# One choice of experts over nine columns instead of two over four and five, and one copy moved in front of the square root, in an attention and mixture-of-experts kernel

## The chip, the cores and the metric

The kernel runs on one core of a Trainium2 chip. Its engines are TensorE (PE in the profile; its weight loads are PEld), VectorE (DVE), ScalarE (ACT), GpSimd (POOL) and SyncE (SP, which here only issues DMAs). Each engine works through its own list of instructions in order and waits for the others by semaphores. The metric is the device time of one execution in microseconds; the number compared is the median over several runs.

## The reference

Linear attention with a norm is followed by a layer of eight experts, in which every expert takes exactly as many tokens as any other:

```
kv  = einsum('bhsd,bhse->bhde', k, v)             # 8 batches, 8 heads, 576 rows, head size 64
out = einsum('bhsd,bhde->bhse', q, kv)
rms = sqrt(mean(out*out, -1) + 1e-6)
x   = (out / rms * g_norm) as (4608, 512)         # tokens x (heads * head size)

logits = x @ w_gate                               # 4608 x 8
for (tok, e) in order of falling logits:          # over all tokens and experts together
    skip if tok is assigned or expert e has 576 tokens
    assigned[tok] = e
out[tokens of e] = relu(x[tokens of e] @ w1[e]) @ w2[e]     # 512 -> 1024 -> 512
```

## The kernel before, in words

**Attention part.** For each batch `prepare` forms kv on TensorE, turns q and appends, behind each head's 64 columns of kv, the 8 columns of kv times w_gate; so one product gives a head's output and its share of the 8 logits. `tiles` then goes through the batch in tiles of 128 tokens. Batches alternate between four tiles and five (the fifth joins the last rows of two batches), so that the 4608 tokens stand in 36 *columns* of 128. For each tile TensorE writes `o_ps` in PSUM (L433), ACT squares it into `sq` (L439; two buffers) and copies it to `o_sb` (L441), and DVE sums the squares of each head into `ms` (L447). Behind the last tile of a batch ACT takes the root `rt` (L450), DVE makes `inv` out of it (L456 to L460), scales the logit shares to `part` (L462) and sums them to the logits `lg` of the batch's columns (L465). GpSimd scales the outputs of a batch into `xo` (L470), except in the last batch, where ACT does it in forty small operations (L475); SyncE writes `xo` to `x_dram`.

In the last batch the copies of tiles 2, 3 and 4 are put off: `keep` goes into the list `held_back` and runs behind the root.

**Choice of experts.** `early` is a generator for a group of columns: clip the logits (L237), take each token's highest (L240), mark and number the expert that has it (L242, L243, L245, L247), and compare the highest logit with 32 candidate thresholds (L303, `over_c`). It yields between these steps. The main loop puts the generator of each batch in the list `choices`, and while it works through the tiles of the next batch it takes steps out of it (`chosen`), by a table of numbers per tile. In the last batch the table is (0, 1, 1, 0, 0), and what remains of the choice of batch 6 is done behind the root by a loop of its own; the choice of batch 7 follows behind its logits.

**Search and experts.** For expert 0 `threshold` counts on TensorE, over all 36 columns, how many tokens lie above each candidate (L576; one weight load and one matmul a column), narrows the threshold on DVE and repeats, four rounds in all. Then the tokens of expert 0 are listed, 14 matmuls that compute nothing needed keep TensorE busy (`warm_ps`, L736), GpSimd gathers the rows of x (L793), TensorE transposes them (L874) and the eight experts follow, with products on TensorE, sums of operands on GpSimd (L896) and sums of results on DVE (L961).

**What sets the order.** Everything up to the first expert is recorded under a manual schedule: each of PE, DVE, ACT and SP gets its instructions in the order in which the code issues them. So where a line stands in the code, and at which tile a generator is stepped, is the engine's order. PSUM of the expert part takes the place of that of the attention part, so its first matmul (L576) waits until the last `o_ps` is copied.

The functions that the change touches, and what calls them:

Of the kernel before, what the change touches and what calls it, by code (L numbers as in the profile page):

```python
# [27 lines left out]
def kernel(  # L28
# [14 lines left out]
    B, H, S, D = q.shape  # L43
# [5 lines left out]
    R = S // HP  # L49
# [25 lines left out]
    def paced(dma):  # L75

        if len(issued) >= 2 * AHEAD:
            tc.add_manual_dep(dma.ins, issued[-AHEAD].name,
                              mybir.DependencyInfo(mybir.DependencyClass.Sync, mybir.DependencyReason.DATA),
                              reason="paced loads")  # L80
        issued.append(dma.ins)
# [146 lines left out]
    def choice(c0=None, c1=GC):  # L228


        cs = slice(c0 or 0, c1)
        n = cs.stop - cs.start
        m, cm, cd = (mx, code_mx, code) if c0 is not None else (small_ps[k] for k in ("mx", "code_mx", "code"))
        if c0 is None:
            nc.vector.tensor_tensor(wl, lg, bc_e(small_ps["shut"]), op=AL.add)
        else:
            nc.vector.tensor_scalar(lg[:, :, cs], in0=lg[:, :, cs], scalar1=bound, scalar2=bottom,  # L237
                                    op0=AL.min, op1=AL.max)
        w = wl if c0 is None else lg
        nc.vector.tensor_reduce(m[:, cs], w[:, :, cs].rearrange("p e c -> p c e"), axis=AXX, op=AL.max)  # L240
        yield
        nc.vector.tensor_tensor(pick[:, :, cs], w[:, :, cs], bc_c(m[:, cs]), op=AL.is_ge)  # L242
        nc.vector.tensor_tensor(pick[:, :, cs], pick[:, :, cs], bc_e(cd, n), op=AL.mult)  # L243
        yield
        nc.vector.tensor_reduce(cm[:, cs], pick[:, :, cs].rearrange("p e c -> p c e"), axis=AXX, op=AL.max)  # L245
        yield
        nc.vector.tensor_tensor(best[:, :, cs], pick[:, :, cs], bc_c(cm[:, cs]), op=AL.is_equal)  # L247
        if c0 is None:
            nc.vector.tensor_tensor(mx, m, gone, op=AL.add)
# [49 lines left out]
    def compare_thirds(over, cand, c0=0, c1=GC):  # L299
        for n in range(3):  # L300
            a, b = max(c0, n * THIRD), min(c1, (n + 1) * THIRD)
            if a < b:
                nc.vector.tensor_tensor(  # L303
                    over[n][:, a - n * THIRD:b - n * THIRD], mx[:, a:b].rearrange("p (c o) -> p c o", o=1).to_broadcast([P, b - a, NCAND]),
                    cand.rearrange("p (o n) -> p o n", o=1).to_broadcast([P, b - a, NCAND]), op=AL.is_ge)

    def early(c0, c1):

        yield from choice(c0, c1)
        yield  # L310
        compare_thirds(over0, cand0, c0, c1)
# [98 lines left out]
    def tiles(c0, rows, last=False):  # L410


        T = len(rows)
        o_sb = att.tile([P, T, H, W], FT, name="o_sb", tag="o_sb", bufs=2)
        xo = att.tile([P, T, H, D], FT, name="xo", tag="xo", bufs=LAG + 1)
        ms = att.tile([P, T * H], FT, name="ms", tag="ms")
        held_back = []
        for t, halves in enumerate(rows):


            in_kv = last and t == 2
            o_ps = psa.tile([P, 2, 512], FT, name="o_ps", tag="kv" if in_kv else "o", bufs=1 if in_kv else 2)
            for r2 in range(NP // 2):
                for l in range(2):
                    for rp in range(2):
                        r = 2 * r2 + rp
                        at = [slice(h * HP, (h + 1) * HP) for h in range(2)]
                        parts = [(slice(0, P), halves[0], 2)] if halves[0][0] == halves[1][0] else [
                            (at[n], half, 1) for n, half in enumerate(halves)]
                        for rows_at, (bn, j), m in parts:  # L430
                            block = R * r + j
                            ks = slice(block % 2 * D, (block % 2 + 1) * D)
                            nc.tensor.matmul(  # L433
                                o_ps[rows_at, rp, (2 * r2 + l) * W:(2 * r2 + l + 1) * W],
                                lhsT=turned_q[bn][ks, l, block // 2:block // 2 + m].rearrange("p x c -> p (x c)"),
                                rhs=kv_of[bn][ks, 2 * r + l], start=True, stop=True)
            o4 = o_ps[:, :, 0:NP * W].rearrange("p b (h w) -> p b h w", w=W)
            sq = att.tile([P, H, D], FT, name="sq", tag="sq")
            nc.scalar.activation(sq.rearrange("p (b h) d -> p b h d", b=2), o4[:, :, :, 0:D], ACT.Square, scale=D ** -0.5)  # L439
            def keep(t=t, o_ps=o_ps):  # L440
                nc.scalar.copy(o_sb[:, t].rearrange("p (b h) w -> p b (h w)", b=2), o_ps[:, :, 0:NP * W])  # L441

            if last and t > 1:
                held_back.append(keep)
            else:
                keep()
            nc.vector.reduce_sum(out=ms[:, t * H:(t + 1) * H], in_=sq, axis=AXX)  # L447
            yield
        rt = att.tile([P, T * H], FT, name="rt", tag="rt")
        nc.scalar.activation(rt, ms, ACT.Sqrt, bias=eps)  # L450
        while last and choices:
            chosen()
        for do in held_back:
            do()
        inv = att.tile([P, T * H], FT, name="inv", tag="inv")
        nc.vector.reciprocal(inv, rt)  # L456

        nc.vector.scalar_tensor_tensor(rt, in0=inv, scalar=-0.5, in1=inv, op0=AL.mult, op1=AL.mult)
        nc.vector.scalar_tensor_tensor(rt, in0=ms, scalar=EPS, in1=rt, op0=AL.add, op1=AL.mult)
        nc.vector.scalar_tensor_tensor(inv, in0=rt, scalar=1.5, in1=inv, op0=AL.add, op1=AL.mult)  # L460
        part = att.tile([P, T * H, E], FT, name="part", tag="part")
        nc.vector.tensor_tensor(  # L462
            part, o_sb[:, :, :, D:W].rearrange("p t h e -> p (t h) e"),
            inv.rearrange("p (a o) -> p a o", o=1).to_broadcast([P, T * H, E]), op=AL.mult)
        nc.vector.reduce_sum(out=lg[:, :, c0:c0 + T].rearrange("p e t -> p t e"),  # L465
                             in_=part.rearrange("p (t h) e -> p t e h", t=T), axis=AXX)

        for t in range(T):
            if c0 + T <= last_own:
                nc.gpsimd.tensor_tensor(xo[:, t], o_sb[:, t, :, 0:D],  # L470
                                        inv[:, t * H:(t + 1) * H].rearrange("p (h o) -> p h o", o=1).to_broadcast([P, H, D]),
                                        op=AL.mult)
            else:
                for h in range(H):
                    late.append(lambda t=t, h=h: nc.scalar.mul(xo[:, t, h], o_sb[:, t, h, 0:D],  # L475
                                                               inv[:, t * H + h:t * H + h + 1]))
        for x in range(0, T, 2):
            y = min(x + 2, T)
            writes.append(lambda x=x, y=y: paced(nc.sync.dma_start(
                x_dram[(c0 + x) * P:(c0 + y) * P, :].rearrange("(t p) f -> p t f", p=P),  # L480
                xo[:, x:y].rearrange("p t h d -> p t (h d)"))))

    def work(b):
        rows = [((b, j), (b, j + 2)) for j in (0, 1, 4, 5)]
        c = b // 2 * R + b % 2 * (R // 2)
        if b % 2:
            rows.append(((b - 1, R - 1), (b, R - 1)))
        column_of.update({c + t: row for t, row in enumerate(rows)})
        yield from tiles(c, rows, b + 1 == B)
        choices.append(early(c, c + len(rows)))  # L490

    choices, column_of = [], {}

    def chosen():

        if choices and next(choices[0], "all") == "all":
            choices.pop(0)
# [830 lines left out]
```

## Time and profile before

| | |
|---|---|
| median of 3 runs | 629.81 us (620.28 to 634.88) |
| profiled execution | 629.0 us, span 627.2 us from first to last instruction |
| granted TensorE clock, mean | 0.956 of full speed |
| PE busy | 591.6 us (94%) |
| PEld busy | 465.3 us (74%) |
| DVE busy | 373.5 us (60%) |
| ACT busy | 179.7 us (29%) |
| POOL busy | 412.9 us (66%) |
| DMA | 91.07 MB, mean 145 GB/s |

The busy shares are means over two unlike parts: the attention part up to about 123 us, and the experts from about 151 us to the end, where TensorE hardly pauses. Between them lies a stretch in which TensorE is mostly idle or does little. A row of the timeline gives the start in us, the duration, the engine, the line, the operation with what it writes and reads, how often, and in brackets how long the engine was idle before it and what ended that. A row of a group gives the busy time in all and the mean in ns of one.

### The profile page before, as it was taken

The page shows a single profiled execution, that of the slowest core. Times are in us where ns is not written, and L with a number is a line of the kernel's source. Part 1 is how long each engine was busy: PE and PEld are TensorE (multiplying, and loading weights), DVE is VectorE, ACT ScalarE, POOL GpSimd, SP SyncE. Part 2 cuts the span into 40 slices and gives each one's busy share as a digit, 9 for nine tenths or more (in the row PEclk, how much of TensorE's full clock was granted, in tenths as well). Part 3 has the DMA queues.
Part 4 walks back from the last instruction along what each step waited for, and adds up shares of the span by engine and source line. Part 5 has one row for each costly group of instructions (what it writes and reads, how often), then busy time and mean ns, then how long its engine had stood idle before and what let it go on. Part 6 is the DMA issues. An engine that isn't in the chain of part 4 may idle for free.

```text
span 627.2 us, 12012 instructions
## 1 busy us (share of the span) xinstructions
PE 591.6 (94%) x4644; PEld 465.3 (74%) x4644; DVE 373.5 (60%) x1172; ACT 179.7 (29%) x387; POOL 412.9 (66%) x367
## 2 busy tenths in 40 slices
PE   6899989638999999999999999999999999999996
PEld 3787877534788678867886787788678867877784
DVE  2535876877887797768746873786383146123511
ACT  1345765742221322122212321322122112212300
POOL 0034455304998989698769696967887799778323
PEclk9858999858999999999999999999999999999998
DMA  8996889827209154075036204610654053002002
GB/s 288 296 319 232 281 289 324 316 86 253 90 8 337 68 199 154 1 245 175 1 135 210 76 0 169 196 56 2 209 202 144 0 182 104 2 1 75 1 1 80
DMA packets 41410, 91.07 MB, mean 145 GB/s; under 512 B 3456, under 2 KB 3456, under 8 KB 41344
## 3 DMA queue, kind: packets, MB, share of 16 engines
q1 hardware_dynamic: 34752, 71.31, 33.3%
q0 software_dynamic: 5888, 18.88, 9.1%
q8 instruction: 39, 0.64, 0.4%
q14 instruction: 27, 0.22, 0.1%
q10 hardware_dynamic: 704, 0.02, 0.1%
HBM read 71.32 MB, written 18.87 MB: 144 GB/s over the span
## 4 chain that ended last, share of the span: by engine, by line
PE 85%; DVE 6%; issue 3%; DMA 2%; POOL 2%; ACT 1%; POOLq 0%; DVEq 0%; ACTq 0%
PE h_ps L966 33%; PE y_ps L1068 31%; PE o_ps L433 5%; PE y_ps L1082 4%; PE kv_ps L345 4%; PE t_ps L874 3%; PE qt_ps L330 2%; DVE ms L447 1%; PE warm_ps L736 1%; DMA v_sb<-in_v_dram 1%; PE given_ps L580 1%; DMA g_col<-in_g_norm_dram 1%; PE given_ps L576 1%; POOL out_dram L883 1%; PE begun_ps L268 0%
## 5 line engine op out<-in xcount | busy, mean ns | idle before, releaser
L966 PE MATMUL h_ps<-xt,w_sb 128*128 128x288 f32 x384 | 101.0, 412 | 0.9 <-ACT xt L877 0.8
L978 ACT ACTIVATE hid<-hid 128x288 f32<-128x288 f32 x128 | 55.7, 445 | 147.4 <-DVE hid L961 141.8
L966 PEld LDWEIGHTS h_ps<-xt,w_sb 128*128 128x128 f32 x384 | 70.8, 190 | 24.8 <-issue 5.7
L961 DVE TENSOR_TENSOR hid<-h_ps,u 128x288 f32<-128x288 f32 x128 | 56.8, 454 | 29.1 <-PE h_ps L966 25.0
L966 PE MATMUL h_ps<-sx,sw 128*128 128x288 f32 x256 | 67.9, 407 | 0.1
L793 POOL DMA_INDIRECT xg<-x_dram,ids x40 | 38.2, 955 | 34.9 <-DVE upper L633 22.6
L1068 PE MATMUL y_ps<-tw,sh 128*128 128x256 f32 x256 | 61.1, 383 | 0.0
L1068 PE MATMUL y_ps<-tw,hid 128*128 128x256 f32 x256 | 60.9, 381 | 0.0
L1068 PE MATMUL y_ps<-w_sb,hid 128*128 128x256 f32 x256 | 59.5, 382 | 0.0
L966 PEld LDWEIGHTS h_ps<-sx,sw 128*128 128x128 f32 x256 | 48.4, 190 | 13.9 <-DVE u L961 0.6
L877 ACT ACTIVATE xt<-t_ps,g_col 128x512 f32<-128x512 f32 (+1 forms) x40 | 25.8, 645 | 110.6 <-PE t_ps L874 110.5
L470 POOL TENSOR_TENSOR xo<-o_sb,inv 128x512 f32<-128x512 f32 x31 | 32.5, 1077 | 30.5 <-ACT sq L439 16.1
L1068 PEld LDWEIGHTS y_ps<-w_sb,hid 128*128 128x128 f32 x256 | 47.4, 190 | 6.4
L1068 PEld LDWEIGHTS y_ps<-tw,sh 128*128 128x128 f32 x256 | 47.3, 190 | 6.1
L1068 PEld LDWEIGHTS y_ps<-tw,hid 128*128 128x128 f32 x256 | 47.1, 190 | 6.0
L961 DVE TENSOR_TENSOR y_sb<-y_ps,u 128x512 f32<-128x512 f32 x24 | 16.5, 690 | 53.5 <-PE y_ps L1068 53.5
L961 DVE TENSOR_TENSOR u<-h_ps,u 128x288 f32<-128x288 f32 x96 | 41.9, 449 | 10.3 <-PE h_ps L966 8.1
L433 PE MATMUL o_ps<-kvx,qt 64*128 64x72 f32 (+1 forms) x640 | 43.7, 286 | 3.4 <-DVE kvx L396 2.4
L433 PEld LDWEIGHTS o_ps<-kvx,qt 64*128 64x128 f32 (+1 forms) x640 | 38.7, 194 | 8.2 <-issue 7.0
L896 POOL TENSOR_TENSOR sh<-hid 128x512 f32<-128x512 f32 x16 | 20.3, 1271 | 32.7 <-ACT hid L978 31.7
L896 POOL TENSOR_TENSOR tw<-w_sb 128x512 f32<-128x512 f32 x32 | 40.0, 1273 | 0.2
L376 POOL COPY kvx<-kv 64x512 f32<-64x512 f32 x16 | 9.8, 611 | 45.7 <-DVE kv L370 45.3
(214 smaller groups left out, 1093.5 us busy)
## 6 DMA issues: line engine op xcount, KB each, us to landing
w_sb<-in_moe_w_dram SPq DMA_DIRECT2D x16, 1024.0 KB, 6.2
w_sb<-in_moe_w_dram SPq DMA_DIRECT2D x8, 2048.0 KB, 13.8
k_sb<-in_k_dram SPq DMA_DIRECT2D x16, 576.0 KB, 5.2
v_sb<-in_v_dram SPq DMA_DIRECT2D x16, 576.0 KB, 5.8
q_sb<-in_q_dram SPq DMA_DIRECT2D x16, 576.0 KB, 6.0
x_dram<-xo SPq DMA_DIRECT2D x16, 512.0 KB, 3.8
x_dram<-xo SPq DMA_DIRECT2D x4, 256.0 KB, 4.4
xg<-x_dram,ids POOLq DMA_INDIRECT x40
```

Source lines behind the costliest of these rows:

```text
L345: nc.tensor.matmul(kv_ps[cs, l, r * D:(r + 1) * D], lhsT=k_sb[ls, r, j, :], rhs=v_sb[ls, r, j, :], start=(j < 2), stop=(j >= R - 2))
L433: nc.tensor.matmul(o_ps[rows_at, rp, (2 * r2 + l) * W:(2 * r2 + l + 1) * W], lhsT=turned_q[bn][ks, l, block // 2:block // 2 + m].rearrange ...
L470: nc.gpsimd.tensor_tensor(xo[:, t], o_sb[:, t, :, 0:D], inv[:, t * H:(t + 1) * H].rearrange("p (h o) -> p h o", o=1).to_broadcast([P, H, D ...
L793: tokens = nc.gpsimd.indirect_dma_start(out=xg[0:nr], out_offset=None, in_=x_dram, in_offset=bass.IndirectOffsetOnAxis(ap=ids[0:nr, n:n + ...
L874: nc.tensor.transpose(t_ps[:, d, 0:nr], xg[0:nr, d * P:(d + 1) * P], ident[0:nr, 0:nr])
L877: nc.scalar.mul(xt[:, :, a:a + nr], t_ps[:, :, 0:nr], g_col)
L896: in_order(nc.gpsimd.tensor_tensor(o, x, y, op=op))
L961: nc.vector.tensor_tensor(o, p_ps, u, op=AL.add)
L966: nc.tensor.matmul(o, lhsT=left[:, d, f * P:(f + 1) * P], rhs=right[:, d], start=d == 0, stop=d == KH - 1)
L978: nc.scalar.activation(h, h, ACT.Relu)
L1068: nc.tensor.matmul(p_ps[:, n], lhsT=left[:, f, n * P:(n + 1) * P], rhs=right[:, f], start=(f == 0), stop=(f == FH - 1))
L1082: nc.tensor.matmul(y_ps[l * nr:(l + 1) * nr], lhsT=hid[:, l * FH + f, a:a + nr], rhs=w2[:, l * FH + f, :], start=(f == 0), stop=(f == FH - 1))
```

## The change

```
@@ in tiles(), behind the loop over the tiles
             nc.vector.reduce_sum(out=ms[:, t * H:(t + 1) * H], in_=sq, axis=AXX)
             yield
+        if held_back:
+            held_back.pop(0)()
         rt = att.tile([P, T * H], FT, name="rt", tag="rt")
         nc.scalar.activation(rt, ms, ACT.Sqrt, bias=eps)
         while last and choices:
@@ in work(b)
         yield from tiles(c, rows, b + 1 == B)
-        choices.append(early(c, c + len(rows)))
+        if b + 2 < B:
+            choices.append(early(c, c + len(rows)))
+        elif b + 1 == B:
+            choices.append(early(c - R // 2, c + len(rows)))
```

`held_back` holds the copies of tiles 2, 3 and 4 of the last batch; the first of them now stands in front of the root. Batch 6 (`b + 2 == B`) no longer leaves a choice behind, so that the steps taken in batch 7 and the loop behind the root find nothing to do, and batch 7 makes one choice over the columns 27 to 35, the four of batch 6 and its own five.

On DVE, in the last batch, the order before runs from the first reduction (`ms`) to the first step of `inv`; `pick`, `code_mx`, `best` and `over_c` are steps of the choice of batch 6:

```order
L447 TENSOR_REDUCE ms<-sq 128x8 x2
L237 TENSOR_SCALAR lg<-lg,bound,bottom 128x8x4
L240 TENSOR_REDUCE mx<-lg 128x4
L447 TENSOR_REDUCE ms<-sq 128x8
L242 TENSOR_TENSOR pick<-lg,mx 128x8x4
L243 TENSOR_TENSOR pick<-pick,code 128x8x4
L447 TENSOR_REDUCE ms<-sq 128x8 x2
L245 TENSOR_REDUCE code_mx<-pick 128x4
L247 TENSOR_TENSOR best<-pick,code_mx 128x8x4
L303 TENSOR_TENSOR over_c<-mx,cand 128x128
L456 RECIPROCAL inv<-rt 128x40
```

The changed kernel, from the same place to the comparison with the candidates (lines from 449 on are two higher in it, later five):

```order
L447 TENSOR_REDUCE ms<-sq 128x8 x5
L458 RECIPROCAL inv<-rt 128x40
...
L464 TENSOR_TENSOR part<-o_sb,inv 128x320
L467 TENSOR_REDUCE lg<-part 128x5x8
L237 TENSOR_SCALAR lg<-lg,bound,bottom 128x8x9
L240 TENSOR_REDUCE mx<-lg 128x9
L242 TENSOR_TENSOR pick<-lg,mx 128x8x9
L243 TENSOR_TENSOR pick<-pick,code 128x8x9
L245 TENSOR_REDUCE code_mx<-pick 128x9
L247 TENSOR_TENSOR best<-pick,code_mx 128x8x9
L303 TENSOR_TENSOR over_c<-mx,cand 128x288
```

The five reductions now stand together, the seven instructions of the four-column choice are gone, and the seven behind `lg` are nine columns wide instead of five.

On ACT, in the last batch, from the third square to the late scaling, before:

```order
L439 ACTIVATE sq<-o_ps 128x512 x3
L450 ACTIVATE rt<-ms,eps 128x40
L441 COPY o_sb<-o_ps 128x576 x3
L475 ACTIVATE xo<-o_sb,inv 128x64 x40
L877 ACTIVATE xt<-t_ps,g_col 128x4x128 x3
```

And in the changed kernel:

```order
L439 ACTIVATE sq<-o_ps 128x512 x3
L441 COPY o_sb<-o_ps 128x576
L452 ACTIVATE rt<-ms,eps 128x40
L441 COPY o_sb<-o_ps 128x576 x2
L477 ACTIVATE xo<-o_sb,inv 128x64 x40
```

One of the three copies has moved from behind the root to in front of it. On TensorE, GpSimd and SyncE the order of the instructions is the same; the counting matmuls of the columns 27 to 30 now need the choice that is made behind `lg`.

More of the change, by code (lines that the diff above doesn't have):

```diff
@@ L448, in tiles @@
             yield
+        if held_back:
+            held_back.pop(0)()
         rt = att.tile([P, T * H], FT, name="rt", tag="rt")
@@ L489, in work @@
         yield from tiles(c, rows, b + 1 == B)
-        choices.append(early(c, c + len(rows)))
+        if b + 2 < B:
+            choices.append(early(c, c + len(rows)))
+        elif b + 1 == B:
+            choices.append(early(c - R // 2, c + len(rows)))
     choices, column_of = [], {}
```

## The prediction

> **What bounds the kernel now.** I read the page first, then the chain of waits, and then the timeline around the end of the attention part, where the edit lies.
>
> ```profile
> PE 85%; DVE 6%; issue 3%; DMA 2%; POOL 2%; ACT 1%; POOLq 0%; DVEq 0%; ACTq 0%
> ```
>
> The chain that ended last is TensorE for 85%, VectorE (DVE) for 6% and ScalarE (ACT) for 1%. So the edit, which changes only the order and widths of DVE and ACT instructions, can act only in a short piece of the span. The timeline shows that piece (columns: start, duration, engine, line, operation, count, and in brackets the idle time before it and what ended it):
>
> ```profile
> 116.17 4.19 POOL L470 TENSOR_TENSOR xo<-o_sb,inv 128x512 f32<-128x512 f32 x4 [3.79 <-ACT sq L439]
> ...
> 116.98 1.27 DVE L447 TENSOR_REDUCE ms<-sq 128x8 f32<-128x512 f32 x2
> ...
> 117.75 1.19 ACT L439 ACTIVATE sq<-o_ps 128x512 f32<-128x512 f32 x2
> ...
> 118.61 0.68 DVE L447 TENSOR_REDUCE ms<-sq 128x8 f32<-128x512 f32 x1
> ...
> 119.38 0.60 ACT L439 ACTIVATE sq<-o_ps 128x512 f32<-128x512 f32 x1 [0.45 <-DVE ms L447]
> 119.44 0.96 DVE L243 TENSOR_TENSOR pick<-pick,code 128x32 f32<-128x32 f32 x1
> ...
> 120.33 1.27 DVE L447 TENSOR_REDUCE ms<-sq 128x8 f32<-128x512 f32 x2
> ...
> 121.63 0.33 ACT L450 ACTIVATE rt<-ms,eps 128x40 f32<-128x40 f32 x1 [1.65 <-DVE ms L447]
> ...
> 121.86 1.70 ACT L441 COPY o_sb<-o_ps 128x576 f32<-128x576 f32 x3
> 122.06 0.40 DVE L456 RECIPROCAL inv<-rt 128x40 f32<-128x40 f32 x1
> ...
> 122.96 0.20 DVE L460 SCALAR_TENSOR_TENSOR inv<-rt,inv 128x40 f32<-128x40 f32 x1
> ...
> 123.60 0.49 DVE L462 TENSOR_TENSOR part<-o_sb,inv 128x320 f32<-128x320 f32 x1 [0.43 <-ACT o_sb L441]
> 123.61 0.98 PE L576 MATMUL given_ps<-best,over_c 128*32 128x8 bf16 x31 [4.93 <-ACT o_sb L441]
> ...
> 126.34 0.32 DVE L303 TENSOR_TENSOR over_c<-mx,cand 128x160 bf16<-128x160 f32 x1
> ...
> 126.71 0.30 PE L576 MATMUL given_ps<-best,over_c 128*32 128x8 bf16 x5 [2.12 <-DVE over_c L303]
> ...
> 128.86 1.43 PE L576 MATMUL given_ps<-best,over_c 128*32 128x8 bf16 x36 [1.44 <-DVE over_c L303]
> ```
>
> Two waits matter. The root (L450) sat 1.65 us until the last of the five reductions of batch 7 came from DVE; that DVE was late because the four-column choice of batch 6 stands between the reductions. Behind the root ACT makes three copies, and `part` (L462) waits 0.43 us for the last. TensorE is idle 4.93 us and then waits 2.12 us more for the choice of the last five columns. From there to the first product of expert 0 the chain is one dependent step after another, and TensorE runs nearly without a gap behind it. What is won or lost up to the matmuls at 126.71 therefore moves the end one for one, unless something on a clock of its own holds it back.
>
> **The reductions come together.** Two squares end at 117.75 + 1.19 = 118.94, so the third is ready at about 118.35 and the fourth at 118.94. Before, the third reduction begins at 118.61 and the last two at 120.33, with the multiply of the choice, 0.96 us long, ahead of them. Its groups by shape:
>
> ```profile
> L243 DVE TENSOR_TENSOR pick<-pick,code 128x32 f32<-128x32 f32 x4 | 2.7, 680 | 0.1
> L243 DVE TENSOR_TENSOR pick<-pick,code 128x40 f32<-128x40 f32 x4 | 0.8, 201 | 0.1
> L243 DVE TENSOR_TENSOR pick<-pick,held_ps 128x288 f32<-128x288 f32 x7 | 3.2, 454 | 0.2
> L240 DVE TENSOR_REDUCE mx<-lg 128x5 f32<-128x40 f32 x4 | 0.9, 224 | 0.1
> L240 DVE TENSOR_REDUCE held_ps<-wl 128x36 f32<-128x288 f32 x7 | 4.7, 672 | 0.2
> L303 DVE TENSOR_TENSOR over_c<-mx,cand 128x160 bf16<-128x160 f32 x3 | 1.0, 319 | 0.0
> L303 DVE TENSOR_TENSOR over_c<-mx,cand 128x384 bf16<-128x384 f32 x9 | 4.5, 554 | 0.1
> ```
>
> With 32 elements it takes 680 ns on average, with 40 only 201. The slow ones lie beside GpSimd's scaling of the tile before: here the multiply ends at 120.40, 0.04 us behind GpSimd's four operations (116.17 + 4.19 = 120.36). The reductions in that stretch keep their 0.68 and 0.64 us, so they aren't held up by it, and without the choice they close up. The third runs from about 118.43 to 119.11. The fifth square needs the buffer of the third and started 0.09 us behind that reduction (118.61 + 0.68 = 119.29, then 119.38); now it runs from 119.20 to 119.80. The fourth reduction fills 119.02 to 119.70, the fifth 119.88 to 120.56. The root follows the last reduction by 0.03 us as it does now (121.60, 121.63): **120.59 in place of 121.63, 1.04 us earlier.**
>
> **The copy in front of the root.** ACT is free at 119.80 and the root can't begin before 120.59. One copy takes 1.70 / 3 = 0.57 us, or at most the 0.63 of a lone one if the overlap is lost, and ends at 120.37 to 120.43: hidden by the fifth reduction, with some 0.2 us to spare. If that cover were gone it would cost the root up to 0.57. Behind the root stand two copies instead of three. They start 0.23 behind the root's start as now and end at 120.82 + 1.13 = 121.95 instead of 123.56. On the other side `inv` ends at 123.16 now and at 122.12 then. The wait of 0.43 for the copies is gone, and what is late next is `inv`: `part` starts at about 122.15 instead of 123.60. **1.45 us earlier.** The late scaling of batch 7 by ACT, the forty small operations behind the copies, and the writes to `x_dram` that it feeds start earlier by as much and are moved past nothing.
>
> **Nine columns at once.** The seven operations of the four-column choice are gone, but none of their time is on the path behind `part`; what is on it grows. From 40 to 288 elements the multiply goes from 201 to 454 ns, 1.0 ns an element; the reduction from 224 to 672, 1.8. Thirty-two more elements cost 0.03 us in each of clip, compare, multiply and equal, and 0.06 in each of the two reductions; the comparison with the candidates gets 128 more at (554 - 319) / 224 = 1.05, 0.13. Sum: 0.25 + 0.13 = **0.38 us later.** (The clip has no wide row of its own; I take the multiply's slope.)
>
> **Nine matmuls behind it instead of five.** The first 27 columns run in TensorE's idle time as soon as the copies free PSUM, at about 122.0. The last nine wait for the choice; at 1.43 / 36 = 0.04 us each, four more are **0.16 us later.**
>
> Sum: -1.45 + 0.38 + 0.16 = **-0.91 us**. Bounds: -1.45 if width cost nothing; -0.3 if the copy weren't hidden (+0.57). The removed wait takes nothing from the work behind, as these rows show:
>
> ```profile
> 133.15 0.33 SPq L479 DMA_DIRECT2D x_dram<-xo  x1
> ...
> 142.99 1.17 POOL L793 DMA_INDIRECT xg<-x_dram,ids  x1 [22.63 <-DVE upper L633]
> ...
> 148.06 0.42 PEld L874 LDWEIGHTS t_ps<-ident,xg 128*128 128x128 f32 x4 [0.58 <-DMA xg<-x_dram,ids]
> ```
>
> The last write of x is issued 9.8 us before the first gather, which waits on DVE; both move forward.
>
> **The TensorE clock.** TensorE's gap ends at about 122.0 instead of 123.61, so the clock's steps must be looked at. Stages cut at the steps (columns: the stage, its length, the busy time of PE, PEld, DVE, ACT and POOL, then granted clock, DMA share, GB/s), then from the timeline an idle time, two like groups of transposes and the 14 warming matmuls ahead of expert 0:
>
> ```profile
> 26.40:29.82 3.42, 1.72 (x74) 1.37 (x72) 2.41 (x9) 0.07 (x1) 0.00 (x0) 1.00 0.90 277
> 29.82:50.29 20.47, 20.47 (x267) 18.10 (x264) 7.84 (x17) 8.26 (x16) 5.40 (x6) 0.50 0.79 265
> ...
> 118.56:121.97 3.41, 0.12 (x8) 0.09 (x1) 3.34 (x9) 1.31 (x4) 1.80 (x2) 1.00 0.82 308
> 121.97:139.04 17.07, 6.21 (x148) 5.13 (x148) 12.61 (x44) 11.15 (x43) 0.00 (x0) 0.50 0.35 134
> 139.04:142.45 3.41, 2.21 (x12) 0.98 (x12) 2.49 (x13) 0.00 (x0) 0.00 (x0) 0.50 0.49 143
> 142.45:145.86 3.41, 3.41 (x10) 1.17 (x9) 0.90 (x4) 0.00 (x0) 2.26 (x3) 0.50 0.68 235
> 145.86:149.27 3.41, 3.01 (x18) 1.47 (x16) 2.51 (x14) 1.20 (x2) 2.67 (x3) 1.00 0.70 181
> 149.27:156.10 6.83, 5.61 (x37) 4.09 (x37) 5.81 (x14) 2.90 (x7) 1.26 (x1) 1.00 0.84 264
> ```
> ```profile
> 28.98 0.91 PE L345 MATMUL kv_ps<-v_sb,k_sb 64*64 64x64 f32 x39 [1.70 <-issue]
> ...
> 40.74 1.11 PE L330 MATMUL qt_ps<-ident,q_sb 128*128 128x128 f32 x4
> ...
> 51.29 0.66 PE L330 MATMUL qt_ps<-ident,q_sb 128*128 128x128 f32 x4
> ...
> 140.64 5.74 PE L736 MATMUL warm_ps<-wide,ones_b 128*128 128x512 bf16 x14
> ```
>
> The clock falls at 29.82 and 121.97 and rises at 50.29 and 145.86. The distances, 20.47, 71.68 and 23.89 us, are 6, 21 and 7 times 3.413: the steps stand on a grid that doesn't follow the program. TensorE is idle in nearly all of 118.56 to 121.97 before and after, so I leave the fall where it is and cost it at nothing.
>
> [...]
>
> **The rivals.**
>
> *The clock rises later* (the one that ends slower). The rise at 145.86 ends the one window that the 14 warming matmuls fill (3.41 of 3.41 busy). Started 0.9 earlier on the same grid, they leave about 0.4 us of it empty and fill the window before to some 3.1. If neither counts, the work of the next window runs at half clock: by the transposes, 1.11 against 0.66, its 3.01 us become 5.06, 2.05 more; if the window after counts neither, 5.61 us of work gain another 3.8. With -0.9 that is **+1.1 to +4.9 us, 630.9 to 634.7.** [...] For it: 2.21 of 3.41 wasn't enough. Against: a second window gets as full as the first gets empty, and on any grid the burst is as long as it was. [...]
>
> *The early slow stretch is absent.* From 29.82 to 50.29 TensorE is busy throughout at half clock, far ahead of the edit. In a run without it this work would take 20.47 x 0.66 / 1.11 = 12.2 us, up to 8.3 less. That reaches from the median to about the lowest run shown (620.28), but no trace of that run shows it. If most runs of the changed kernel were like that: **620.6**, by no merit of the edit.
>
> *The clock holds* through 122 to 139, against the reading above: the three full rounds of counting matmuls (1.43 each) could shrink by half at best, 2.1 us: **626.8**. [...]
>
> *Nothing arrives,* because a transfer sets the start of expert 0: **629.8**. Against it, the gather waits on DVE, and the transposes on the gather. That the edit does nothing is excluded: the order shows both moves.
>
> **How the numbers follow.** The profiled execution took 629.0 us (span 627.2), 0.8 below the median of 629.81. Less 0.9, it gives 628.1, and the median 628.9; I take the median's. The forecast gets 0.64, with an own range of 628.3 to 629.5 (-1.5 to -0.3); the later rise 0.13, no early stretch 0.15, the held clock 0.03, nothing 0.05. The runs shown spread from 620.28 to 634.88, sixteen times the sum, so the range is theirs less 0.9, which also holds all the rivals: 619.4 to 634.0 (the very end of the later rise lies outside). Two per cent, 12.6 us, is about what a measurement of this kernel can tell from no change, and no case reaches it on either side: within gets 0.93. Faster keeps 0.04: the early stretch absent, the held clock and the sum come to 11.3 us together. Slower keeps 0.03: the later rise at its longest, in a run like the slowest shown, gives 634.0 + 5.9 = 639.9, 10.1 above the median.
>
> **What would show it.** Right: five reductions in a row, the root at about 120.6 on the same count, no wait of `part` for `o_sb`, the nine-column choice about 0.4 us longer than the five-column one, first expert product about 0.9 us earlier. Wrong: ACT's copy ending behind the last reduction; reductions slowed beside GpSimd; the clock rising later than some 5.2 us after the first warming matmul.

## The result, and the profile after

| | before | after |
|---|---|---|
| median of 20 runs each | 624.71 us (620.28 to 634.88) | 620.18 us (615.36 to 626.39) |
| profiled execution | 629.0 us, span 627.2 | 620.8 us, span 619.0 |
| granted TensorE clock, mean | 0.956 | 0.977 |
| PE busy | 591.6 us | 583.0 us |

The ratio is 0.9939 (95% interval 0.9912 to 0.9966): 3.8 us faster, between 2.1 and 5.5. That is within two per cent, and four times the forecast of 0.91 us. The intervals given here leave out executions more than 1.5% above the fastest of their kernel; where a mean or a fit is made below over all executions, the text says so.

The edit did what it says. This is the timeline of the changed kernel from the last `o_ps` products to the first count (start, duration, engine, line, operation, count, idle time before and what ended it):

```profile
107.31 4.46 PE L433 MATMUL o_ps<-kvx,qt 64*128 64x72 f32 x96 [0.31 <-DVE kvx L396]
...
109.26 4.14 POOL L472 TENSOR_TENSOR xo<-o_sb,inv 128x512 f32<-128x512 f32 x4 [3.79 <-ACT sq L439]
...
110.07 3.49 DVE L447 TENSOR_REDUCE ms<-sq 128x8 f32<-128x512 f32 x5
...
112.24 0.60 ACT L439 ACTIVATE sq<-o_ps 128x512 f32<-128x512 f32 x1 [0.22 <-DVE ms L447]
112.74 0.63 ACT L441 COPY o_sb<-o_ps 128x576 f32<-128x576 f32 x1
113.59 0.33 ACT L452 ACTIVATE rt<-ms,eps 128x40 f32<-128x40 f32 x1 [0.22 <-DVE ms L447]
113.83 1.16 ACT L441 COPY o_sb<-o_ps 128x576 f32<-128x576 f32 x2
...
114.93 0.20 DVE L462 SCALAR_TENSOR_TENSOR inv<-rt,inv 128x40 f32<-128x40 f32 x1
115.04 0.87 PE L581 MATMUL given_ps<-best,over_c 128*32 128x8 bf16 x27 [3.27 <-ACT o_sb L441]
...
115.23 0.49 DVE L464 TENSOR_TENSOR part<-o_sb,inv 128x320 f32<-128x320 f32 x1
...
116.53 0.32 DVE L237 TENSOR_SCALAR lg<-lg,bound,bottom 128x72 f32<-128x72 f32 x1
...
118.69 0.41 PE L581 MATMUL given_ps<-best,over_c 128*32 128x8 bf16 x9 [2.78 <-DVE over_c L303]
...
119.35 0.16 PE L598 MATMUL k_ps<-full_b,ones_b 32*128 32x8 bf16 x1 [0.25 <-DVE full_b L596]
...
143.07 1.24 PE L971 MATMUL h_ps<-xt,w_sb 128*128 128x288 f32 x4 [0.78 <-ACT xt L882]
```

The five reductions of batch 7 stand in one row. The copy ends at 113.37, still ahead of the root, and the root waits 0.22 us for DVE in place of 1.65. `part` carries no wait for `o_sb` any more. The count of the last nine columns starts 2.16 us after the clip (118.69 - 116.53); with five columns it was 1.82 (126.71 - 124.89).

Counted from the first reduction of batch 7, so that what happened earlier drops out:

| us from the first reduction to | before | after | difference | forecast |
|---|---|---|---|---|
| the root | 4.65 | 3.52 | -1.13 | -1.04 |
| `part` | 6.62 | 5.16 | -1.46 | -1.45 |
| `k_ps`, the first step behind the first count | 10.28 | 9.28 | -1.00 | -0.91 |

So the edit is worth 1.0 us up to the first count, and the profiled executions differ by 8.2 in span. Where is the rest? Cut each span at two points: the end of the last `o_ps` product (107.31 + 4.46 = 111.77 after, 114.22 + 4.46 = 118.68 before) and the first `h_ps` product. The piece behind the second is 475.99 us before and 475.93 after. The stretch between them, in which the edit lies, is 32.53 and 31.30; 0.2 us of this difference lie behind the count. The attention part ahead of it is 118.68 and 111.77: **6.9 of the 8.2 us come from work that the edit doesn't touch.** The windows of 20 us tell why (length, busy time of PE, PEld, DVE, ACT and POOL with counts, granted clock, DMA share, GB/s). Before:

```profile
0.00:20.00 20.00, 14.21 (x181) 8.12 (x181) 5.53 (x34) 2.65 (x4) 2.13 (x10) 0.83 0.88 295
20.00:40.00 20.00, 18.18 (x307) 15.79 (x309) 11.21 (x43) 8.91 (x19) 1.98 (x4) 0.74 0.91 300
40.00:60.00 20.00, 19.32 (x378) 16.78 (x374) 10.94 (x26) 10.61 (x21) 8.37 (x10) 0.74 0.74 249
```

After:

```profile
0.00:20.00 20.00, 15.15 (x223) 9.71 (x223) 6.69 (x41) 4.08 (x8) 2.44 (x10) 1.00 0.88 296
20.00:40.00 20.00, 19.22 (x485) 16.78 (x486) 15.24 (x47) 12.99 (x25) 6.30 (x8) 1.00 0.93 305
40.00:60.00 20.00, 18.41 (x417) 15.88 (x411) 14.52 (x37) 12.06 (x25) 10.78 (x12) 1.00 0.92 311
```

The granted clock was 0.83, 0.74 and 0.74 in the first 60 us before and 1.00 in all three after. TensorE is about as busy in both (18.18 and 19.22 us between 20 and 40), but got through 307 matmuls in the one and 485 in the other. The time at half clock in the attention part, from the stages cut at the clock's steps, is 27.3 us before and 6.8 after. Both are whole numbers of 3.41 us (8 and 2). In a part where the two kernels issue the same instructions until batch 7, this can be chance; the experiments had to show whether it is.

With less half clock the chain of waits of the changed kernel runs through transfers more (DMA 2% before, 8% now, most of it the load of q) and through PE less. By engine, then by line:

```profile
PE 79%; DMA 8%; DVE 7%; issue 2%; POOL 2%; ACT 1%; POOLq 0%; DVEq 0%; ACTq 0%; SPq 0%
PE h_ps L971 33%; PE y_ps L1073 31%; DMA q_sb<-in_q_dram 5%; PE y_ps L1087 4%; PE t_ps L879 3%; PE o_ps L433 2%; PE kv_ps L345 2%; PE qt_ps L330 1%; DMA v_sb<-in_v_dram 1%; DVE ms L447 1%; PE given_ps L585 1%; PE given_ps L581 1%; DMA g_col<-in_g_norm_dram 1%; DMA x_dram<-xo 1%; DMA xg<-x_dram,ids 1%
```

### The profile page after: what moved, and what is told of

Same layout as the page of the kernel before. It is cut to its first block, busy times and chain, and to the rows that moved or that the text cites. A ratio compares the mean times of both kernels' runs of the same rounds, so it can differ in the third digit from the quotient of the medians.

```text
span 619.0 us, 12005 instructions
## 1 busy us (share of the span) xinstructions
PE 583.0 (94%) x4644; PEld 459.2 (74%) x4644; DVE 372.1 (60%) x1165; ACT 179.5 (29%) x387; POOL 412.2 (67%) x367
## 4 chain that ended last, share of the span: by engine, by line
PE 79%; DMA 8%; DVE 7%; issue 2%; POOL 2%; ACT 1%; POOLq 0%; DVEq 0%; ACTq 0%; SPq 0%
PE h_ps L971 33%; PE y_ps L1073 31%; DMA q_sb<-in_q_dram 5%; PE y_ps L1087 4%; PE t_ps L879 3%; PE o_ps L433 2%; PE kv_ps L345 2%; PE qt_ps L330 1%; DMA v_sb<-in_v_dram 1%; DVE ms L447 1%; PE given_ps L585 1%; PE given_ps L581 1%; DMA g_col<-in_g_norm_dram 1%; DMA x_dram<-xo 1%; DMA xg<-x_dram,ids 1%
## 5 line engine op out<-in xcount | busy, mean ns | idle before, releaser
L798 POOL DMA_INDIRECT xg<-x_dram,ids x40 | 38.1, 952 | 34.0 <-DVE upper L638 21.7
L433 PE MATMUL o_ps<-kvx,qt 64*128 64x72 f32 (+1 forms) x640 | 40.0, 272 | 2.7 <-DVE kvx L396 2.6
L901 POOL TENSOR_TENSOR sh<-hid 128x512 f32<-128x512 f32 x16 | 20.3, 1268 | 33.1 <-ACT hid L983 31.9
L433 PEld LDWEIGHTS o_ps<-kvx,qt 64*128 64x128 f32 (+1 forms) x640 | 35.3, 180 | 7.1 <-issue 5.7
L888 POOL DMA_INDIRECT out_dram<-y_sb,outs x32 | 31.3, 977 | 11.7 <-issue 10.3
## 6 DMA issues: line engine op xcount, KB each, us to landing
w_sb<-in_moe_w_dram SPq DMA_DIRECT2D x8, 2048.0 KB, 13.7
```

Source lines behind the costliest of these rows:

```text
L433: nc.tensor.matmul(o_ps[rows_at, rp, (2 * r2 + l) * W:(2 * r2 + l + 1) * W], lhsT=turned_q[bn][ks, l, block // 2:block // 2 + m].rearrange ...
L798: tokens = nc.gpsimd.indirect_dma_start(out=xg[0:nr], out_offset=None, in_=x_dram, in_offset=bass.IndirectOffsetOnAxis(ap=ids[0:nr, n:n + ...
L888: put = nc.gpsimd.indirect_dma_start(out=out, out_offset=bass.IndirectOffsetOnAxis(ap=ids_of[t][0:nr, n:n + 1], axis=0), in_=y_sb[0:nr, :] ...
L901: in_order(nc.gpsimd.tensor_tensor(o, x, y, op=op))
```

## The experiments

Two theories. *The edit's 0.9 to 1.0 us is all of it*, and the rest of the first ratio is when the clock falls in the attention part. *The edit is worth 3.8 us*, by some way in which it also calms the clock or the loads. Rivals of the prediction (a rise that comes later, a clock that holds, a step that gives nothing) are tested beside them.

**Both kernels again, unchanged**, several times over:

> The kernel before, instruction for instruction, timed against itself. Theory 1 (the edit saves its 0.9 us between the last attention product and expert 0, and the rest of the measured 3.8 us is a difference between executions): ratio 1.000, and its interval shows how wide chance is here; an interval that reaches below 0.997 would already hold most of the unexplained 2.9 us. Theory 2 (the attention part as a whole runs faster in the changed program): ratio 1.000 with an interval inside 0.997 to 1.003.

> The changed kernel again. Theory 1: ratio about 0.9985 (0.9 of 625 us), surely above 0.996; from the end of the last o_ps product to the first h_ps product of expert 0 about 31.3 to 31.7 us against 32.5 before. Theory 2: ratio again near 0.994, with the gain in the time up to the last o_ps product, where no instruction differs.

> The changed kernel a third time, for the question whether its first ratio of 0.9939 belongs to it. Theory 1 (0.9 to 1.0 us saved locally, the rest is when TensorE's clock falls in the attention part, by chance): ratio 0.9985, the same within the interval as the second timing's 0.9986; its profile has 31.2 to 31.7 us from the last o_ps product to the first h_ps product and 476 us behind. Theory 2 (something of the whole program): ratio 0.994.

> The changed kernel a fourth time, for more executions beside the kernel before on one chip. Theory 1 (1 us saved locally, when the clock falls in the attention part is chance): over all four timings the difference at an equal mean granted clock stays at 1.0 us less, and this timing's ratio lies anywhere from 0.994 to 1.003. Theory 2 (the changed program spends less time at half clock in the attention part): its mean granted clock is again above that of the kernel before by about 0.005, as in the first timing.

> The kernel before against itself a second time. Theory 1: ratio within 0.996 to 1.004 of 1.000; the first self-comparison gave 0.9977. Its profile has 32.5 to 33.1 us from the last o_ps product to the first h_ps product and 476 us behind, with the end of the attention part between 110 and 121 us as the clock falls.

> As e8_after_fourth; the two together tell how far two timings of one kernel on one chip lie apart. Theory 1: they differ by up to 0.4%, and both lie at 0.9985 within their intervals. Theory 2: both near 0.994.

Measured, against the kernel before in the same session:

| run | kernel | ratio (95%) | median, us | attention part (half clock in it) | stretch |
|---|---|---|---|---|---|
| first | before | | 624.71 | 118.68 (27.3) | 32.53 |
| second | before | 0.9977 (0.9938 to 1.0015) | 622.12 | 120.35 (30.7) | 33.11 |
| third | before | 1.0001 (0.9963 to 1.0039) | 623.30 | 114.78 (17.1) | 32.66 |
| first | changed | 0.9939 (0.9912 to 0.9966) | 620.18 | 111.77 (6.8) | 31.30 |
| second | changed | 0.9986 (0.9951 to 1.0020) | 621.66 | 111.14 (13.7) | 31.35 |
| third | changed | 0.9972 (0.9930 to 1.0014) | 620.51 | 117.35 (27.3) | 31.29 |
| fourth | changed | 0.9952 (0.9916 to 0.9988) | 622.09 | 115.87 (20.5) | 31.09 |
| fifth | changed | 0.9946 (0.9908 to 0.9985) | 618.72 | 108.15 (3.4) | 31.20 |

The last two columns are of the one profiled execution of each. The stretch is 32.5 to 33.1 us before and 31.1 to 31.35 in the changed kernel, with no overlap; the times from the first reduction, as in the table above, come out within 0.02 us in each of them. So the stretch differs by 1.2 to 2.0 us, where those times give 1.0. From `k_ps` to the issue of the third gather (L793, later L798) both kernels take the same time within 0.05 us; the rest is how long that gather takes from its issue to the first transpose of its rows, on which the first `h_ps` product waits: 4.08, 4.69 and 4.25 us in the three profiles of the kernel before, 3.68 to 3.92 in the five of the changed one, but 3.93 and 4.72 in two of one kernel (the copy alone, below). Whether the edit shortens it, these runs don't show.

The attention part varies by 6 us in the one kernel and by 9 in the other, and goes with the half clock in it. The third profile of the changed kernel had as much half clock as the first of the kernel before, and an attention part 1.3 us shorter (117.35 against 118.68). The falls begin at 13, 30, 47, 64 to 74 and 95 to 102 us, at other places in other executions.

Each execution's time is also listed with its mean granted clock, which gives its half-clock time as 2 x (1 - clock) x time, since the stages cut at the clock's steps were granted 1.00 or 0.50. Over all such executions of these kernels and of those below, 259 without the outliers named at the end, one line fits: 0.34 us of time for each us of half clock (0.32 to 0.36), with a level for each kernel. At equal half-clock time the changed kernel (67 executions) lies **0.88 us below the kernel before (135), ± 0.53**. Without the first timing of the changed kernel it is 0.87 ± 0.59. The 20 executions of that first timing had 33.1 us of half clock on average, where those of the kernel before in all later sessions had 40.8; 7.7 x 0.34 = some 2.6 us of the first ratio's 3.8 go with that. (This is an estimate: the clocks of the kernel before in the first session aren't listed. On average its executions there took 625.4 us, 2.2 more than in the later sessions, and those of the changed kernel 619.7, 2.2 less.) The plain means are 621.27 and 623.28, 2.0 us apart (± 1.3); the rest of that is half-clock time, 37.5 us on average against 40.8, 3.3 ± 3.5. The fourth and fifth timing, at 0.9952 and 0.9946, lie nearer to the 0.994 of the second theory than to the 0.9985 of the first. But their means are 1.7 and 2.4 us below the kernel before of their session with 3.0 and 4.6 us less half clock, which leaves 0.7 and 0.8 us at equal clock; and in the session of the third timing the changed kernel had more half clock than the kernel before (44.3 us against 39.2). So the first theory holds at equal clock. Whether the last 1.1 us (3.3 x 0.34) between the plain means is chance or the edit's, these runs can't say.

**The merged choice alone**, without the copy ahead of the root:

```
-        if held_back:
-            held_back.pop(0)()
         rt = att.tile([P, T * H], FT, name="rt", tag="rt")
```

> Only the one choice over nine columns, the three copies all behind the root. By the sum: root 1.04 us earlier, three copies behind it end at 122.5 in place of 123.56 on the profile's count, so part 1.04 earlier, less 0.38 and 0.16: 0.5 us less than before between the last o_ps product and the last counting matmul of the first round, with a wait of part for o_sb of about 0.4 us. Theory 1: ratio 0.999. Theory 2: if the shorter DVE program is what matters, ratio near 0.994 as for the whole change.

Measured: 0.9951 (0.9907 to 0.9995), median 621.35. Its timeline:

```profile
108.71 3.50 DVE L447 TENSOR_REDUCE ms<-sq 128x8 f32<-128x512 f32 x5
...
112.24 0.33 ACT L450 ACTIVATE rt<-ms,eps 128x40 f32<-128x40 f32 x1 [0.75 <-DVE ms L447]
112.47 1.70 ACT L441 COPY o_sb<-o_ps 128x576 f32<-128x576 f32 x3
...
114.21 0.49 DVE L462 TENSOR_TENSOR part<-o_sb,inv 128x320 f32<-128x320 f32 x1 [0.43 <-ACT o_sb L441]
```

The root comes 3.53 us after the first reduction, as in the whole change, so its gain is all the merge's. `part` still waits 0.43 us for the third copy and comes at 5.50 instead of 5.16. `k_ps` is 0.66 us earlier than before. The ratio taken alone would speak for the second theory; over all twelve executions the mean is 622.4 us, 1.1 below the kernel before of its session (623.5), with 1.0 us less half clock.

**The copy alone**, with the two choices as before (timed once, and executed once more for a second profile):

```
-        if b + 2 < B:
-            choices.append(early(c, c + len(rows)))
-        elif b + 1 == B:
-            choices.append(early(c - R // 2, c + len(rows)))
+        choices.append(early(c, c + len(rows)))
```

> Only the first of the three copies in front of the root; the choices stay as before. By the sum: root as before, two copies end 0.57 earlier, part then waits for inv: 0.4 us less in the same stretch, and no wait of part for o_sb. Theory 1: ratio 0.9993. Theory 2 (number of DVE instructions): ratio 1.000, since none is gone.

> The copy alone once more, for a profile in which the last batch runs at full clock as in the profile before. By the sum: first reduction of batch 7 to the root 4.65 us as before, part 0.4 us earlier than before (6.2 instead of 6.6 behind the first reduction), no wait for o_sb. If the last batch runs at half clock again, the reductions are spread and the multiply of the four-column choice takes its 0.2 us outside GpSimd's operations.

Measured: 1.0004 (0.9963 to 1.0045), median 624.49; the second profile's execution 624.37. In the profile of the timed run the last 96 `o_ps` products ran at half clock (8.28 us, where the others have 4.46), so the reductions came apart and the times from the first of them can't be compared. The second profile has full clock there:

```profile
111.37 4.19 POOL L472 TENSOR_TENSOR xo<-o_sb,inv 128x512 f32<-128x512 f32 x4 [3.79 <-ACT sq L439]
...
113.37 0.29 DVE L237 TENSOR_SCALAR lg<-lg,bound,bottom 128x32 f32<-128x32 f32 x1
...
114.64 0.97 DVE L243 TENSOR_TENSOR pick<-pick,code 128x32 f32<-128x32 f32 x1
...
116.83 0.33 ACT L452 ACTIVATE rt<-ms,eps 128x40 f32<-128x40 f32 x1 [1.12 <-DVE ms L447]
117.06 1.16 ACT L441 COPY o_sb<-o_ps 128x576 f32<-128x576 f32 x2
...
118.47 0.49 DVE L464 TENSOR_TENSOR part<-o_sb,inv 128x320 f32<-128x320 f32 x1
```

The root stays at 4.65; the wait of `part` is gone (6.29 instead of 6.62), and `k_ps` is 0.32 us earlier. The two halves of the change add up: 0.66 + 0.32 = 0.98, against 1.00 together. At equal half-clock time the kernels lie 0.9 ± 1.05 (merge) and 0.4 ± 1.1 (copy) below the kernel before: in the direction of these times, though there are too few executions to prove either.

The profile of the timed run had a use of its own. There GpSimd's operations lie elsewhere, and with them the slow DVE operation:

```profile
105.04 8.28 PE L433 MATMUL o_ps<-kvx,qt 64*128 64x72 f32 x96 [0.22 <-DVE kvx L396]
...
106.97 4.14 POOL L472 TENSOR_TENSOR xo<-o_sb,inv 128x512 f32<-128x512 f32 x4 [4.74 <-DVE inv L462]
...
110.08 1.07 DVE L237 TENSOR_SCALAR lg<-lg,bound,bottom 128x32 f32<-128x32 f32 x1
...
112.12 0.19 DVE L243 TENSOR_TENSOR pick<-pick,code 128x32 f32<-128x32 f32 x1
```

The multiply L243, 0.97 us long beside GpSimd in the second profile, takes 0.19 when GpSimd has ended at 111.11, and it is the clip (L237), 0.29 us in the second profile, that now takes 1.07 and ends 0.04 us behind GpSimd.

**The clock held from the end of the attention part to expert 0**, by matmuls that compute nothing needed, added to the changed kernel:

```
@@ in tiles(), ahead of the copy and the root of the last batch
+        if last:
+            hold_ps = psa.tile([P, 4, P], FT, name="hold_ps", tag="tr", bufs=2)
+            for _ in range(13):
+                nc.tensor.matmul(hold_ps..., lhsT=ones_b, rhs=wide, start=True, stop=True)
@@ in threshold(), first round behind column 26, and behind each k_ps
+                    if s == 0 and c == GC - R - 1:
+                        warm(10)
+                warm(5 if s + 1 < NSTEP else 8)
@@ ahead of expert 0
-            warm(14)
+            warm(22)
```

> The changed kernel with matmuls that compute nothing needed in TensorE's idle places behind attention: 13 behind the last o_ps product, 10 in front of the last nine counting matmuls, 5 after each counting round and 8 after the last, and 22 instead of 14 ahead of the gather. If the half clock costs something in this stretch, a full counting round falls from 3.27 us towards 2.6 and the stretch from the last o_ps product to the first h_ps product from 31.3 to 29 or 30 us. If the stretch is DVE and gather alone, it stays at 31.3 although the granted clock is 1.00, and the third rival of the prediction was worth nothing. The whole: 2 us less than the changed kernel at best, too little for its timing.

Measured: 1.0015 (0.9964 to 1.0066), median 622.91. The stretch, as one window of each kernel; changed, then held:

```profile
111.77:143.07 31.30, 14.69 (x189) 9.06 (x189) 22.73 (x82) 14.48 (x49) 6.54 (x7) 0.67 0.60 209
```
```profile
109.99:141.15 31.16, 25.16 (x243) 13.09 (x243) 22.72 (x82) 14.49 (x49) 6.54 (x7) 1.00 0.55 190
```

The clock was granted in full throughout, and the stretch is 31.16 us, among the 31.09 to 31.35 of the changed kernel's five profiles. A full round of counting, one row of the held kernel's timeline, is no shorter than the 1.43 us that it took at half clock:

```profile
119.17 1.42 PE L585 MATMUL given_ps<-best,over_c 128*32 128x8 bf16 x36 [0.25 <-DVE over_c L303]
```

The half clock between the attention part and the experts costs nothing that can be seen here; in the changed kernel TensorE waits for DVE in 11.1 of its 20.5 us. So the rival by which the clock holds had a price of nothing, not of 2.1 us, and a mean granted clock counts here time that costs nothing: that is why this kernel lies 6.3 us *above* the line of the kernel before, and 7.1 above that of the changed one (the 20.5 us of half clock, six windows, that it lacks there would be 7.0 at 0.34).

**One matmul of 512 columns ahead of each attention tile**, computing nothing needed, to see what the falls there cost:

```
             o_ps = psa.tile([P, 2, 512], FT, name="o_ps", ...)
+            nc.tensor.matmul(o_ps[:, 0], lhsT=ones_b, rhs=wide, start=True, stop=True)
```

> The changed kernel with one matmul of 512 columns that computes nothing needed ahead of each of the 36 attention tiles (0.21 us each at full clock, 7.8 us of TensorE in all). If the spread between executions comes from the clock falling when TensorE does too little in the attention part, the mean granted clock rises above 0.975 and the spread of the times shrinks; a profile without a fall ends the attention part at 110 to 111 us. If TensorE has no room there, the attention part ends about 5 us later instead and the kernel is 0.5 to 1% slower.

Measured: 0.9978 (0.9951 to 1.0005), median 622.15, range 619.76 to 624.02. The whole attention part of the profiled execution, changed kernel and then this one:

```profile
0.00:111.77 111.77, 98.37 (x2117) 82.31 (x2117) 70.51 (x210) 59.69 (x118) 41.76 (x54) 0.97 0.90 303
```
```profile
0.00:112.53 112.53, 105.78 (x2153) 83.13 (x2153) 70.99 (x211) 60.06 (x118) 43.44 (x55) 1.00 0.90 306
```

The clock never fell there in this execution. Its mean clock of 0.983 is the highest of the twelve; the lowest is 0.973, so that some of the others may have had a fall there. The standard deviation of the times went from 4.8 us in the changed kernel (3.8 in the kernel before) to 1.2: **it is the falls in the attention part that scatter the times.** But PE is busy 7.4 us longer there, though at full clock, and at equal half-clock time the kernel lies 3.9 us above the changed one (3.04 + 0.88). What the clock gives, the added work takes.

**The same ahead of every second tile**, and not in the last batch:

```
+            if t % 2 == 0 and not last:
+                nc.tensor.matmul(o_ps[:, 0], lhsT=ones_b, rhs=wide, start=True, stop=True)
```

> The changed kernel with the unneeded matmul ahead of every second attention tile only, and none in the last batch (17 instead of 36, 3.6 us of TensorE). From the runs so far: at an equal mean clock the 36 cost 3.9 us over the changed kernel, so 17 cost about 1.9; if they are enough to keep the clock up, the half-clock time falls from 37 to some 24 us, worth 13 x 0.34 = 4.5 us. Then the median is 617 to 618.5 us, below both kernels, with a spread under 5 us. If every second tile is too little, the falls stay in part of the executions and the median is 620 to 622 with a wide spread.

Measured: 0.9971 (0.9938 to 1.0005), median 621.08, lowest 617.22. Its profile still had 23.9 us of half clock in an attention part of 118.05. The lower level that was hoped for wasn't reached in most executions; no version here is clearly faster than the changed kernel.

## Why the prediction was right and where it failed

- **The reductions come together: right.** The root came 1.13 us earlier for 1.04. The 0.09 more lie in the row of reductions, which is closer than reckoned: 3.49 us for five (forecast: 116.98 to 120.56, 3.58). One reading on the way was wrong and cost nothing: of the four slow multiplies of 32 elements only the last lies beside GpSimd's scaling, the other three (0.58 to 0.59 us) beside its copies into `kvx` (L376).
- **The copy in front of the root: right.** It ends 0.22 us ahead of the root (forecast: some 0.2), and the copy's share of the gain, 0.32 us, shows alone.
- **`part`: right**, 1.46 us for 1.45, with no wait for copies.
- **Nine columns and nine matmuls: right in size.** 0.34 us for 0.38, and 0.41 - 0.30 = 0.11 for 0.16. The sum of -0.91 came out as -1.00 in the profiles, counted from the first reduction, and as -0.88 ± 0.53 by the times at equal half-clock time.
- **The later rise: fell.** The clock rose at 136.30 on the same grid of 3.41 us, at the end of the one window that the warming matmuls fill (132.89 to 136.30 in the trace), 3.56 us after the first of them (132.74) and not more than 5.2. No run shows a busy share of a window that brings the rise or keeps it away: in the profile before, TensorE was busy in all of each of the six windows from 29.82 to 50.29, and the clock rose behind the last of them only. The half clock between the attention part and the experts was 6 or 7 windows in every profile but two (the clock held; the timed run of the copy alone, where the clock had fallen earlier), and it cost nothing that showed.
- **The clock holds: fell.** It fell at 115.81, though TensorE's gap was 3.27 us instead of 4.93; and held by force it gave nothing (31.16 us against 31.09 to 31.35). With the gap filled the clock was granted in full (1.00), but a length of gap that decides the fall no run shows: in the window ahead of the fall at 29.82 before, the longest was 1.70 us. That the drop costs time is what this stretch doesn't bear out.
- **Nothing arrives: fell.** Counted from the first reduction, the gathers were issued 1.0 us earlier, as the count was, and the first `h_ps` product came earlier too (stretch 32.5 to 33.1 against 31.1 to 31.35).
- **The early slow stretch absent: this is where it went wrong.** The step that failed is the one under "How the numbers follow". It took the median of three runs (629.81) and one execution with 27.3 us of half clock in the attention part as what the kernel does, and set the half clock down as one stretch that is either there (as in the forecast) or absent (chance 0.15). Even in that execution there were two: the clock had fallen at 12.73 too, until 19.56. The runs showed falls at changing places in every profile of the two kernels, 3 to 31 us of half clock in the attention part, and times that follow. Over 20 runs the median before was 624.71, 5.1 us below the base. Of the ratio's 3.8 us 0.9 is the edit; most of the other 2.9 goes with less half clock in those executions (some 2.6 by the line). That the median landed within 0.5 us of this rival's 620.6 is luck and no proof of its picture: half of its drop is in the base, not in the change.
- The range of 619.4 to 634.0 held 620.18, at its edge; the own range of 628.3 to 629.5 was far too narrow, since it bounded the costs of the edit and not the base.

## What to carry to other kernels

Cost a small edit from the rows around it, and check it there too: counted from an event just ahead of the edit, one profiled execution showed 1.00 us, while 20 timed runs of each kernel gave 2.1 to 5.5. Before a median is taken as a base, look whether the granted clock of the executions scatters; if it does, compare at equal half-clock time. Clock that was lost while TensorE waited for another engine cost nothing here (a stretch of 31.16 us with the clock held, 31.09 to 31.35 without), and the work added to keep it up in the attention part cost as much as it saved (a mean of 622.0 us with it, 621.27 without).

## What the runs showed of the hardware that was not expected

- **TensorE can be at half clock while the profile calls it busy, and where the clock falls changes from run to run.** The stage 29.82 to 50.29 before had PE busy in all of its 20.47 us, at half clock. In other executions the same instructions ran at full clock (in the changed kernel's profile 1.00 over its first 60 us). In the attention parts of all 14 profiles each fall stands at the end of a window of the grid, 3.41 us, in which PE was busy for 1.0 to 2.7 us; but windows with as little as 1.6 us passed without a fall, so the busy time doesn't decide a fall by itself. With one bf16 matmul of 128 x 512 a tile, 0.38 us each, the profiled execution had no fall there. What sets the clock these runs don't show; the profile's busy time alone it is not.
- **Half clock costs 0.34 us for each us of it**, on average over the kernel: about 0.4 in the attention part (a line through the eight profiles of the table), nothing that showed between it and the experts. (Whether loads cover a part of the loss there, these runs don't show; the chain of waits has 2% DMA before and 8% in the changed kernel.)
- **Some DVE operations that start beside one of GpSimd's end only with it.** Three times the slow operation ended 0.04 to 0.05 us behind the last of GpSimd's four: the multiply at 120.40 before and at 115.61 in the second profile of the copy alone, the clip at 111.15 in the first. The reductions among the same operations kept their 0.67 us. What makes the multiply and the clip wait and not the reductions, these runs don't show. What the clip costs depends on where it starts: in the 14 profiles the four-column clip starts 45 times beside one of GpSimd's scalings. 40 times 0.32 us or more of that scaling was left, and the clip ended 0.036 to 0.050 us behind it; five times 0.15 us or less was left, and the clip took 0.29 to 0.30 us, as it does alone. So the 1.07 us above is a clip that started 0.01 us behind the start of a scaling, and the 0.29 one that started 0.14 us ahead of the end of another.
- **Rare executions are far off**, and nothing here explains them: 862.58 and 762.47 us at a mean clock of 0.65 and 0.745, and 2103.97, 2908.35 and 3367.69 us at a clock of 1.00, five executions of 264. They are left out of the fit.
